# Turning attention outputs and q by DMA transposes in place of TensorE transposes

## The chip, the cores and the metric

The kernel runs on one core of one Trainium2 chip. The metric is the device time of one execution in microseconds; before the change three runs gave 191.22, 191.66 and 192.19 us, median 191.66 us. The profiled execution spans 190.9 us on the core.

## The reference: block attention with sorted keys, then a top-1 mixture of experts

There are B = 4 batches, H = 8 heads, S = 768 positions and head dimension D = 64. The sequence is cut into 8 blocks of 96. A small matrix P per batch and head (8 x 8, normalised five times over rows and columns) mixes the blocks of k and v. Each block of q then attends to the mixed block of the same number. The attention output, laid out as x of 3072 tokens by 512 features, goes to 8 experts, of which each token uses the best one.

```python
for _ in range(5):
    P = P - np.max(P, axis=-1, keepdims=True)
    P = np.exp(P)
    P = P / (np.sum(P, axis=-1, keepdims=True) + 1e-09)
    P = P / (np.sum(P, axis=-2, keepdims=True) + 1e-09)
k_sorted = np.einsum('bhij,bhjcd->bhicd', P, k_b)
v_sorted = np.einsum('bhij,bhjcd->bhicd', P, v_b)
scores = scale * np.matmul(q_b, k_sb.transpose(0, 1, 2, 4, 3))
attn = softmax(scores)
x = np.matmul(attn, v_sb)            # as (3072, 512)
logits = x @ w_gate                  # (3072, 8)
e = argmax(logits); gate = softmax(logits)[e]
out = gate * (np.maximum(x @ w1[e], 0.0) @ w2[e])
```

## The kernel before, in words

All matmul operands are bf16; the loads on GpSimd's DMA queue turn the fp32 inputs into bf16 on the way. TensorE does every matrix product and every transpose into PSUM, and VectorE or ScalarE copies results from PSUM to SBUF (`evac`, lines 254 to 258, where `engine`, line 246, chooses the engine with the smaller planned load).

The work of one batch has these parts.

- `turn_q` (line 265) turns q. Each batch has two pieces of 128 partitions (head, block and half block) by 24 x 64 columns. Twelve TensorE transposes of 128 x 128 per piece (line 269) fill a PSUM tile, and two copies per piece move it into `qT`.
- `sort_k` (line 291) and `sort_v` (line 312) apply P to k and v by matmuls with the matrices `pdiag`, and copy the results into `ksT` and `vs`. `sort_v` does two batches at a time.
- `attention` (line 375) goes over the 8 blocks. `scores` (line 333) does 16 matmuls of 64 rows by 48 columns into PSUM and one exponential on ScalarE over 768 columns into one of three `ex` tiles. `values` (line 355) does 8 matmuls with `ex` as the weights, and VectorE divides by the row sums into the tile `xo` (96 positions by 512 features; the pool has three of these). `turn` (line 372) does four TensorE transposes (line 378), and a copy puts the result into `xT`, features on partitions, for the whole batch. These three steps are staggered: in one pass of the loop block t gets its scores, block t - 1 its values and block t - 2 its turn. For the first four blocks of batch 0, four more transposes of the identity matrix (line 383) are issued as filler, which keep TensorE running.
- `route` (line 488) multiplies `xT` of a batch with the gate weights (line 493) and computes the expert's index and the gate on VectorE and ScalarE. It is called one pass after the last block's turn.
- `experts` (line 548) takes `xT` of a batch through the one expert whose weights were fetched. It does two halves of 384 tokens with 8 groups of 4 matmuls each (line 558), each followed by a relu from PSUM on VectorE or ScalarE, then 6 tiles of 128 tokens with 8 matmuls each (line 571), each followed by a scaled copy and a store to HBM from SyncE's queue (line 587).

The expert of a batch is guessed ahead from the sums of v (`predict`, `fetch`), so the weights are on their way long before the routing is known; a loop at the end redoes tokens for which the guess was wrong, and isn't entered when there are none.

The order of the instructions is written out by the program itself. Every part is a Python generator that yields an estimate in ns of the TensorE time it has issued (`T_Q`, `T_K`, `T_S`, ... in lines 262 and 263). `merge` (line 18) draws from two streams in proportion to their expected lengths: the experts of batch b, and beside them the q turn, k sort and attention of batch b + 1 (lines 652 to 669). Each engine then works through its own instructions in that order. Before the loop, `HEAD` passes of batch 0's attention are issued alone (line 632).

PSUM is shared by three tags with two buffers each: `s` (q, sorted k, scores, turned outputs), `v` (values) and `f` (experts and the small things). The q pieces have four buffers (`in_q`).

On GpSimd's DMA queue the order of loads is: q, v and k of batch 0 and v of batch 1; the first expert's weights; q and k of batch 1; the second expert's weights; v of batches 2 and 3; q and k of batch 2; and, from `look_ahead` (line 638) in the second pass of the main loop, the weights, q and k for the rest.

Of the kernel before, what the change touches and what calls it, by code (L numbers as in the profile page):

```python
# [9 lines left out]
BF16 = mybir.dt.bfloat16  # L10
# [31 lines left out]
def kernel(  # L42
# [11 lines left out]
    nc = tc.nc  # L54
# [7 lines left out]
    P = 128  # L62
# [64 lines left out]

    qT = [consts.tile([P, P, QC], BF16, name=f"qT{i}") for i in range(2)]  # L130
    ksT = [consts.tile([P, P * CW + 8], BF16, name=f"ksT{i}") for i in range(2)]
    ks3 = [t[:, :P * CW].rearrange("p (h c) -> p h c", c=CW) for t in ksT]
    vs = consts.tile([P, 2, HI, D + 2], BF16)
# [120 lines left out]
    def evac(dst, src, n, on=None):  # L254
        if (on or engine(n)) == "v":
            nc.vector.tensor_copy(dst, src)  # L256
        else:
            nc.scalar.copy(dst, src)  # L258

    T_Q, T_K, T_V, T_S, T_A, T_T = 680.0, 56.0, 89.0, 320.0, 380.0, 190.0
    T_1, T_2 = 650.0, 214.0

    def turn_q(b, on=None):
        for p in range(2):
            ps = psp.tile([P, 2, 8, P], BF16, tag="s")
            for u in range(CP // 2):
                nc.tensor.transpose(  # L269
                    out=ps[:, u // 6, u % 6, :],  # L270
                    in_=q_pieces[b][p][:, 2 * u:2 * u + 2, :].rearrange(
                        "p c d -> p (c d)"),
                    identity=ident)
            for g in range(2):
                c0 = p * (CP // 2) + g * 6
                evac(qT[b % 2][:, :, c0:c0 + 6],
                     ps[:, g, :6].rearrange("p c h -> p h c"), 768, on)
            yield T_Q

    def parts(total, alone):  # L280

# [9 lines left out]
    def sort_k(b):  # L291
        for w0, n, ps in parts(HC + 1, b == 0):
            for u in range(n):
                nc.tensor.matmul(  # L294
                    out=ps[:, u, :],
                    lhsT=k_in[b % 2][:, w0 + u:w0 + u + 2, :].rearrange(
                        "p c d -> p (c d)"),
                    rhs=pdiag[b].rearrange("p h i u -> p (h i u)"),
                    start=(u % 4 == 0), stop=(u % 4 == 3 or u == n - 1),
                    skip_group_check=True)  # L300
            evac(ks3[b % 2][:, :, w0:w0 + n],
                 ps[:, :n].rearrange("p c h -> p h c"), n * P)
            yield n * T_K
# [19 lines left out]
                 ps[:, :n].rearrange("p d h -> p h d"), n * P)  # L323
            yield n * T_V

    L_QK = 2 * T_Q + (HC + 1) * T_K
    L_V = D * T_V


# [3 lines left out]
    def scores(b, i):  # L333
        sc = psp.tile([P, 2, 512], F32, tag="s")
        for h in range(H):
            hi = h * NB + i
            for par in range(2):
                rows = slice(par * D, (par + 1) * D)
                k0 = hi * P + 1 - par
                nc.tensor.matmul(  # L340
                    out=sc[:, par, h * HC:(h + 1) * HC],
                    lhsT=ksT[b % 2][rows, k0:k0 + P],
                    rhs=qT[b % 2][rows, hi * U:(hi + 1) * U, :].rearrange(
                        "p u c -> p (u c)"),
                    start=(h == 0), stop=(h == H - 1), skip_group_check=True)
        ex = exs[n_ex[0] % len(exs)]
        n_ex[0] += 1
        nc.scalar.activation(  # L348
            ex[:, :H * BLK].rearrange("p (h t c) -> p t h c", t=2, c=HC),
            sc[:, :, :H * HC].rearrange("p t (h c) -> p t h c", c=HC),  # L350
            ACT.Exp, scale=scale)
        load["s"] += 810
        return ex
# [16 lines left out]
        return xo  # L370

    def turn(b, i, xo, fill):
        xf = xo.rearrange("p t g d -> p (t g d)")
        tp = psp.tile([P, 8, P], BF16, tag="f" if b == 0 else "s")
        tx = tp[:, :3].rearrange("p a c -> p (a c)").rearrange(
            "p (m c) -> p m c", c=BLK)
        for dc in range(DC):
            nc.tensor.transpose(out=tx[:, dc, :],  # L378
                                in_=xf[:, dc * P:(dc + 1) * P],
                                identity=ident[:BLK, :BLK])  # L380

        for f in range(fill):
            nc.tensor.transpose(out=tp[:, 4 + f, :], in_=ident, identity=ident)
        evac(xTs[b][:, :, i * BLK:(i + 1) * BLK].rearrange(
                 "p m (c t) -> p m c t", t=2),
             tx.rearrange("p m (t c) -> p m c t", t=2), 384)

    def attention(batches, fill):

        blocks = [(b, i) for b in batches for i in range(NB)]  # L390
        n = len(blocks)
        exq, xoq = {}, {}
        late = []
        for t in range(n + 3):
            if t < n:
                exq[t] = scores(*blocks[t])
                yield T_S
            if late:
                late.pop()()
            if 1 <= t <= n:  # L400
                xoq[t - 1] = values(*blocks[t - 1], exq.pop(t - 1))
                yield T_A
            if 2 <= t < n + 2:
                b, i = blocks[t - 2]
                if i == 0:
                    xT = keep.tile([P, DC, S], BF16, tag="xT")
                    xTs[b] = xT
                turn(b, i, xoq.pop(t - 2), fill if i < NB // 2 else 0)
                if i == NB - 1:
                    late.append(lambda b=b: route(b))  # L410
                yield T_T

# [133 lines left out]
    def experts(b, gwb, w, add):  # L548
        w1t, w2t = w
        xT = xTs[b]  # L550
        hTs = []
        for half in range(2):
            hT = ffn.tile([P, FC, NH], BF16, tag="hT")
            hTs.append(hT)
            for fc in range(FC):
                ps = psp.tile([P, NH], F32, tag="f")
                for dc in range(DC):
                    nc.tensor.matmul(  # L558
                        out=ps, lhsT=w1t[:, dc, fc * P:(fc + 1) * P],
                        rhs=xT[:, dc, half * NH:(half + 1) * NH],  # L560
                        start=(dc == 0), stop=(dc == DC - 1))
                if engine(NH) == "v":
                    nc.vector.tensor_scalar_max(hT[:, fc, :], ps, 0.0)  # L563
                else:
                    nc.scalar.activation(hT[:, fc, :], ps, ACT.Relu)  # L565
                yield T_1
        for t in range(NTB):
            hT, s = hTs[t // SUB], t % SUB
            ps = psp.tile([P, MD], F32, tag="f")
            for fc in range(FC):  # L570
                nc.tensor.matmul(  # L571
                    out=ps, lhsT=hT[:, fc, s * P:(s + 1) * P],
                    rhs=w2t[:, fc, :], start=(fc == 0), stop=(fc == FC - 1))
                if fc % 3 == 2:
                    yield 3 * T_2
            rows = slice(b * S + t * P, b * S + (t + 1) * P)
            o = ffn.tile([P, MD], F32, tag="o", bufs=3)
            if add:
                nc.sync.dma_start(out=o, in_=out[rows])
                nc.vector.scalar_tensor_tensor(  # L580
                    out=o, in0=ps, scalar=gwb[:, t:t + 1], in1=o,
                    op0=ALU.mult, op1=ALU.add)
            elif engine(MD) == "s":
                nc.scalar.activation(o, ps, ACT.Copy, scale=gwb[:, t:t + 1])  # L584
            else:
                nc.vector.tensor_scalar_mul(o, ps, gwb[:, t:t + 1])  # L586
            nc.sync.dma_start(out=out[rows], in_=o)
            yield 2 * T_2

    L_EXPERTS = 2 * FC * (T_1 + SUB * T_2)  # L590
    chosen = [None] * B
    tops = [None] * NPAIR

    def expert(b):
        yield from experts(b, gw[:, b], chosen[b], add=False)

    L_ATTEND = NB * (T_S + T_A + T_T)
    AHEAD = 0.88

    def attend(b, fill=0):  # L600
# [28 lines left out]
        load_k(2, p)  # L629
    idle_turns(1)  # L630
    main = attend(0, fill=4)
    HEAD = 3 * 6
    for _ in range(HEAD):
        next(main)
    spread(rep, 1, B)
# [16 lines left out]
    for b in range(B):  # L652
        steps, n = [], 0.0
        if b == 0:
            steps.append(lambda: main)
            n += L_ATTEND * 0.5
        if b + 1 < B:
            steps += [lambda: turn_q(b + 1), lambda: sort_k(b + 1)]
            n += L_QK
            if b + 1 == 2:  # L660
                steps.insert(0, look_ahead)
                steps.append(lambda: sort_v(1))
                n += L_V + 66 * 30.0
            steps.append(lambda: attend(b + 1))
            n += L_ATTEND
            merge((L_EXPERTS, expert(b)), (n / AHEAD, chain(*steps)))
        else:
            rest_i = count_others()
            run(expert(b))


    rv = nc.values_load(rest_i[0:1, 0:1], min_val=0, max_val=N)
    with tc.If(rv > 0):
        cur = consts.tile([P, 1], F32)
        nc.vector.memset(cur, float(E))
# [39 lines left out]
```

The softmax here doesn't subtract the row's maximum and nothing guards it: scores larger than these inputs give would overflow.

## Time and profile before

| what | us |
|---|---|
| device time, median of three | 191.66 |
| span of the profiled execution | 190.9 |
| TensorE busy | 158.1 (83%) |
| VectorE busy | 107.1 (56%) |
| ScalarE busy | 100.3 (53%) |
| GpSimd busy | 25.4 (13%) |
| loads on GpSimd's queue | 17.84 MB |
| stores and the first small load on SyncE's queue | 6.30 MB |

A busy time is the time in which at least one instruction of the engine ran. Matmuls overlap in TensorE's pipeline, so the mean of one matmul is longer than the step from one to the next. The chain that ended last is followed back from the last instruction, at each step to whatever released it, and its shares tell where a saved microsecond is one.

The stages by time: up to 31 us the inputs arrive, P is computed, and v and k of batch 0 are sorted. From 31.7 us the first blocks of attention run; the first expert matmul starts at 42.4 us. From there to 163.8 us the experts of batches 0, 1 and 2 run interleaved with the attention of the next batch (the first expert matmul of batch 1 is at 83.7 us), and the last 27 us are the experts of batch 3 alone.

### The profile page before, as it was taken

Reading aid. Unit: us, or ns where it says so; the run is one execution under the profiler, and the core shown is the slowest. Engines: PE = TensorE matmul, PEld = TensorE weight load, DVE = VectorE, ACT = ScalarE, POOL = GpSimd, SP = SyncE. Lnnn points to the kernel's source line nnn. Section 1 sums busy time; section 2 is a strip of 40 time slices with the busy share of each in tenths; the row PEclk is TensorE's granted clock in tenths of the full one; section 3 lists DMA queues with packets and bytes.
Section 4 is the critical chain, followed back from the end, with each engine's and each line's share of the span. In section 5 each row is a group of like instructions: output and inputs, shape, how many; then the busy total and the mean of one; then the engine's idle time right before and its main releaser. Section 6 shows DMA issues by size and latency. Waiting matters only on the chain.

```text
span 190.9 us, 4797 instructions
## 1 busy us (share of the span) xinstructions
PE 158.1 (83%) x2023; PEld 105.5 (55%) x2023; DVE 107.1 (56%) x308; ACT 100.3 (53%) x159; POOL 25.4 (13%) x51
## 2 busy tenths in 40 slices
PE   0342986987896999997889989989989999999990
PEld 0232975764664656555668845546756555555430
DVE  5870675879466767414754756763648656442210
ACT  5160478573775566533566466645776574434111
POOL 7960074122100000002900000000000000000000
PEclk9999999579999999999999999999999999999999
DMA  4999149999999993140999999713000122300332
GB/s 58 168 211 204 25 45 203 189 216 209 209 217 215 207 179 112 58 165 5 149 193 203 212 211 227 188 55 113 0 0 3 58 83 85 112 0 0 111 138 96
DMA packets 13211, 24.50 MB, mean 128 GB/s; under 512 B 1409, under 2 KB 5505, under 8 KB 13185
## 3 DMA queue, kind: packets, MB, share of 16 engines
q0 software_dynamic: 9680, 17.84, 52.2%
q1 hardware_dynamic: 3504, 6.30, 9.0%
q8 instruction: 18, 0.29, 0.6%
q14 instruction: 9, 0.07, 0.1%
HBM read 35.68 MB, written 6.29 MB: 220 GB/s over the span
## 4 chain that ended last, share of the span: by engine, by line
PE 62%; DVE 16%; ACT 9%; DMA 7%; issue 2%; POOL 1%; ACTq 0%; POOLq 0%
PE ps L571 19%; PE ps L558 18%; DMA v_in<-in_v_dram 7%; PE ps L316 6%; DVE xo L367 5%; PE sc L340 4%; PE ps L294 4%; PE av L361 4%; ACT ksT L258 3%; PE tp L378 2%; DVE ksT L256 2%; ACT qT L258 2%; DVE o L586 2%; DVE qT L256 1%; PE ps L439 1%
## 5 line engine op out<-in xcount | busy, mean ns | idle before, releaser
L558 PE MATMUL ps<-xT,w1t 128*128 128x384 bf16 x256 | 50.5, 326 | 1.4 <-ACT xT L258 0.9
L571 PE MATMUL ps<-w2t,hT 128*128 128x512 bf16 x192 | 48.7, 379 | 0.2
L563 DVE TENSOR_SCALAR hT<-ps 128x384 bf16<-128x384 f32 x37 | 20.6, 556 | 29.2 <-PE ps L558 29.0
L558 PEld LDWEIGHTS <-w1t 128*128 128x128 bf16 x256 | 23.0, 98 | 15.0 <-issue 4.0
L348 ACT ACTIVATE ex<-sc 128x768 bf16<-128x768 f32 x32 | 25.8, 814 | 10.0 <-PE sc L340 9.7
L367 DVE TENSOR_TENSOR xo<-av,rec 96x256 bf16<-96x256 f32 x64 | 26.9, 421 | 2.2
L571 PEld LDWEIGHTS <-hT 128*128 128x128 bf16 x192 | 15.8, 97 | 14.1 <-DVE sh L501 1.2
L565 ACT ACTIVATE hT<-ps 128x384 bf16<-128x384 f32 x27 | 13.3, 492 | 18.5 <-PE ps L558 18.4
L584 ACT ACTIVATE o<-ps,gw 128x512 f32<-128x512 f32 x15 | 10.3, 685 | 16.6 <-PE ps L571 15.4
L258 ACT COPY xT<-tp 128x384 bf16<-128x384 bf16 x29 | 13.8, 477 | 9.8 <-PE tp L378 8.4
L361 PE MATMUL av<-vs,ex 128*128 128x65 bf16 x256 | 15.6, 200 | 3.7 <-DVE rec L366 1.4
L258 ACT CAST ksT<-ps 128x1024 bf16<-128x1024 f32 (+2 forms) x18 | 16.1, 921 | 3.2 <-PE ps L294 3.0
L361 PEld LDWEIGHTS <-ex 128*128 128x128 bf16 x256 | 11.9, 101 | 9.7 <-DVE xo L367 2.7
L294 PE MATMUL ps<-pdiag,k_in 128*128 128x128 bf16 x196 | 14.8, 219 | 2.4 <-ACT vs L258 0.7
L294 PEld LDWEIGHTS <-k_in 128*128 128x128 bf16 x196 | 12.6, 98 | 5.3 <-issue 3.2
L269 PE MATMUL ps<-ident,t 128*128 128x128 bf16 x96 | 7.9, 242 | 8.7 <-DMA t<-in_q_dram 8.7
L366 DVE RECIPROCAL rec<-av 96x4 f32<-96x4 f32 x64 | 11.0, 171 | 6.9 <-PE av L361 6.7
L586 DVE TENSOR_SCALAR o<-ps,gw 128x512 f32<-128x512 f32 x9 | 6.8, 751 | 14.3 <-PE ps L571 14.3
L340 PE MATMUL sc<-qT,ksT 64*128 64x48 bf16 x512 | 12.1, 184 | 2.8 <-DVE ksT L256 1.3
L316 PEld LDWEIGHTS <-v_in 128*128 128x128 bf16 x128 | 13.5, 194 | 1.6 <-issue 0.9
L316 PE MATMUL ps<-pdiag_v,v_in 128*128 128x128 bf16 x128 | 13.6, 268 | 0.8 <-ACT ksT L258 0.8
L340 PEld LDWEIGHTS <-ksT 64*128 64x128 bf16 x512 | 8.8, 95 | 9.4 <-issue 6.7
(96 smaller groups left out, 148.4 us busy)
## 6 DMA issues: line engine op xcount, KB each, us to landing
out_dram<-o SPq DMA_DIRECT2D x24, 256.0 KB, 2.0
w1t<-in_moe_w_dram POOLq DMA_DIRECT2D x4, 1024.0 KB, 15.7
w2t<-in_moe_w_dram POOLq DMA_DIRECT2D x4, 1024.0 KB, 21.1
t<-in_q_dram POOLq DMA_DIRECT2D x8, 384.0 KB, 15.6
v_in<-in_v_dram POOLq DMA_DIRECT2D x4, 768.0 KB, 18.9
k_in<-in_k_dram POOLq DMA_DIRECT2D x8, 384.0 KB, 18.3
sn<-in_sort_net_dram SPq DMA_DIRECT2D x1, 8.0 KB, 1.5
wg<-in_moe_w_gate_dram POOLq DMA_DIRECT2D x1, 8.0 KB, 3.8
```

The source lines that it names most:

```text
L258: nc.scalar.copy(dst, src)
L294: nc.tensor.matmul(out=ps[:, u, :], lhsT=k_in[b % 2][:, w0 + u:w0 + u + 2, :].rearrange("p c d -> p (c d)"), rhs=pdiag[b].rearrange("p h i ...
L316: nc.tensor.matmul(out=ps[:, u], lhsT=v_in[:, :, :, d0 + u].rearrange("p u c -> p (u c)"), rhs=pdiag_v[g].rearrange("p h i -> p (h i)"), s ...
L340: nc.tensor.matmul(out=sc[:, par, h * HC:(h + 1) * HC], lhsT=ksT[b % 2][rows, k0:k0 + P], rhs=qT[b % 2][rows, hi * U:(hi + 1) * U, :].rear ...
L348: nc.scalar.activation(ex[:, :H * BLK].rearrange("p (h t c) -> p t h c", t=2, c=HC), sc[:, :, :H * HC].rearrange("p t (h c) -> p t h c", c ...
L361: nc.tensor.matmul(out=av[:, g, :], lhsT=ex[:, h * BLK:h * BLK + P], rhs=vs[:, b % 2, h * NB + i, :D + 1], start=(g == 0), stop=(g == 3), ...
L366: nc.vector.reciprocal(rec, av[:BLK, :, D:D + 1])
L367: nc.vector.tensor_mul(xo[:, half], av[:BLK, :, :D], rec.to_broadcast([BLK, 4, D]))
L558: nc.tensor.matmul(out=ps, lhsT=w1t[:, dc, fc * P:(fc + 1) * P], rhs=xT[:, dc, half * NH:(half + 1) * NH], start=(dc == 0), stop=(dc == DC ...
L563: nc.vector.tensor_scalar_max(hT[:, fc, :], ps, 0.0)
L565: nc.scalar.activation(hT[:, fc, :], ps, ACT.Relu)
L571: nc.tensor.matmul(out=ps, lhsT=hT[:, fc, s * P:(s + 1) * P], rhs=w2t[:, fc, :], start=(fc == 0), stop=(fc == FC - 1))
```

## The change

The attention outputs and the q of batches 1 to 3 are turned by transposing DMAs, from SBUF to SBUF on SyncE's queue, which also carries the output stores. It is meant to take the transposes off TensorE and the copies out of PSUM off VectorE and ScalarE. The q of batch 0 is still turned on TensorE.

[...] `qT` becomes `[P, QC, P]`, and the scores' right operand is read from it with a step. The exponential writes `ex` with the two halves of a block interleaved, so that the rows of `xo` come out in the order of the tokens. The turn yields no time of its own, the estimates `T_S` and `T_A` are a little smaller, and the routing moves from the end of the attention into the middle of the experts, after the first half.

```diff
-    qT = [consts.tile([P, P, QC], BF16, name=f"qT{i}") for i in range(2)]
+    qT = [consts.tile([P, QC, P], BF16, name=f"qT{i}") for i in range(2)]
...
-    T_Q, T_K, T_V, T_S, T_A, T_T = 680.0, 56.0, 89.0, 320.0, 380.0, 190.0
+    T_Q, T_K, T_V, T_S, T_A = 680.0, 56.0, 89.0, 300.0, 310.0
...
+    def flip_q(b):
+        for p in range(2):
+            c0 = p * (CP // 2)
+            nc.sync.dma_start_transpose(
+                out=qT[b % 2][:, c0:c0 + CP // 2, :],
+                in_=q_pieces[b][p].rearrange("p c d -> p (c d)"))
...
-                    rhs=qT[b % 2][rows, hi * U:(hi + 1) * U, :].rearrange(
-                        "p u c -> p (u c)"),
+                    rhs=qT[b % 2][rows, :, hi * U:(hi + 1) * U].rearrange(
+                        "p c u -> p u c"),
...
-            ex[:, :H * BLK].rearrange("p (h t c) -> p t h c", t=2, c=HC),
-            sc[:, :, :H * HC].rearrange("p t (h c) -> p t h c", c=HC),
+            ex[:, :H * BLK].rearrange("p (h c t) -> p h c t", h=H, t=2),
+            sc[:, :, :H * HC].rearrange("p t (h c) -> p h c t", h=H),
...
     def turn(b, i, xo, fill):
-        xf = xo.rearrange("p t g d -> p (t g d)")
-        tp = psp.tile([P, 8, P], BF16, tag="f" if b == 0 else "s")
...
-        for dc in range(DC):
-            nc.tensor.transpose(out=tx[:, dc, :],
-                                in_=xf[:, dc * P:(dc + 1) * P],
-                                identity=ident[:BLK, :BLK])
-
-        for f in range(fill):
-            nc.tensor.transpose(out=tp[:, 4 + f, :], in_=ident, identity=ident)
-        evac(xTs[b][:, :, i * BLK:(i + 1) * BLK].rearrange(
-                 "p m (c t) -> p m c t", t=2),
-             tx.rearrange("p m (t c) -> p m c t", t=2), 384)
+        nc.sync.dma_start_transpose(
+            out=xTs[b][:, :, i * BLK:(i + 1) * BLK],
+            in_=xo.rearrange("p t g d -> p (t g d)"))
+
+        if fill:
+            tp = psp.tile([P, 8, P], BF16, tag="f")
+            for f in range(fill):
+                nc.tensor.transpose(out=tp[:, f, :], in_=ident, identity=ident)
...
+            if half == 0 and not add:
+                route(b)
+                if b == B - 1:
+                    others.append(count_others())
+                yield 700.0
...
-    HEAD = 3 * 6
+    HEAD = 2 * 6
...
-            steps += [lambda: turn_q(b + 1), lambda: sort_k(b + 1)]
-            n += L_QK
+            flip_q(b + 1)
+            steps.append(lambda: sort_k(b + 1))
+            n += L_K
```

On SyncE's queue the order in the changed program is: the turns of blocks 0 to 3 of batch 0, the two halves of batch 1's q, the turns of blocks 4 to 7 of batch 0, then stores and turns in the order of the merge, with the q of batch 2 behind the last store of batch 0's experts and the q of batch 3 behind the last store of batch 1's.

## Prediction

> **What bounds the kernel now.** I first read the page's forty slices (each a fortieth of the span), the shares of the chain that ended last, then the groups with shapes kept apart.
>
> ```profile
> PE   0342986987896999997889989989989999999990
> PEclk9999999579999999999999999999999999999999
> DMA  4999149999999993140999999713000122300332
> ...
> PE 62%; DVE 16%; ACT 9%; DMA 7%; issue 2%; POOL 1%; ACTq 0%; POOLq 0%
> ```
>
> From about 42 us on TensorE is 90% busy or nearly so in almost every slice, at full clock, and it holds 62% of the chain. Instructions taken off TensorE there are worth nearly their own time. The DMA row is the other thing to see: it is full from about 31 to 72 us and from about 93 to 124 us, and almost empty elsewhere.
>
> ```profile
> L378 PE MATMUL tp<-ident,xo 96*128 96x96 bf16 x128 | 11.5, 214 | 0.9 <-ACT hT L565 0.4 <-DVE xo L367 0.3 <-DVE hT L563 0.2
> L269 PE MATMUL ps<-ident,t 128*128 128x128 bf16 x96 | 7.9, 242 | 8.7 <-DMA t<-in_q_dram 8.7
> L258 ACT COPY xT<-tp 128x384 bf16<-128x384 bf16 x29 | 13.8, 477 | 9.8 <-PE tp L378 8.4 <-PE tp L383 1.1
> L258 ACT COPY qT<-ps 128x768 bf16<-128x768 bf16 x12 | 9.2, 807 | 4.9 <-PE ps L269 2.6 <-DVE qT L256 2.3
> ```
>
> These are the rows that go. The means (214, 242 ns) are of pipelined matmuls and overlap; what one costs in a stream is read from the chain, whose columns are start, length, what:
>
> ```profile
> 48.10 0.34 PE tp L378 x4
> 48.47 0.49 ACT xT L258
> ...
> 49.64 0.59 PE lg L493 x24
> ...
> 130.63 0.67 PE ps L269 x12
> ```
>
> Twelve q transposes hold TensorE for 0.67 us, 56 ns each. Four output transposes take 0.34 us with their drain, about 0.2 us in a stream. And line 493, the gate of batch 0, can start at 49.64 only when the last copy into `xT` is done: all eight blocks of a batch must be turned before its routing.
>
> The last view is what the 16 DMA engines did in the half microsecond from 116.5 us (queue, packets, MB, share of the engines' time), and then, from the microsecond around its issue at 112.58 us, how long an output store took to land.
>
> ```profile
> q0 software_dynamic: 48, 0.05, 57.7%
> q1 hardware_dynamic: 44, 0.09, 52.8%
> ```
>
> ```profile
> out_dram<-o SPq DMA_DIRECT2D x1, 256.0 KB, 7.1
> ```
>
> Queue 0 carries the loads, queue 1 SyncE's stores. While both are active they take turns almost packet by packet (48 against 44). That store landed after 7.1 us; the median of the 24 stores is 2.0 us. Its first packet moved only 3.5 us after the issue.
>
> **What the skill says.** The Trainium skill, "DMA: Bandwidth & Descriptors", section "Queues, rings and completion order", says that each DMA engine goes round its rings at packet granularity. The trace agrees: 48 and 44. The same page, sections "SDMA does more than copy" and "DMA Transpose (X-bar)", describes the transpose in tiles with 256-byte source rows, 16 partitions by 128 columns at least. No run here shows one. Its section "Latency and other measured facts" gives 261 GB/s where the middle dimension isn't contiguous, which it puts down to descriptors that are not joined to 4 KB. I take that one, since our tiles are cut out of longer rows. Unmeasured here too. "SBUF — State Buffer", section "Door 1: The DMA port swizzle", says reads that touch a new 16-byte line each time pay a penalty; the trace has one such read, the strided weight loads of line 316, 194 ns against 98 ns for contiguous ones.
>
> **The change part by part.**
>
> *Removed from TensorE.* 72 q transposes (batches 1 to 3) at 56 ns: 4.0 us. 128 output transposes, 32 groups at 0.2 us: 6.4 us. The 16 filler transposes stay. Off ScalarE and VectorE: 29 x 477 + 3 x 549 ns = 15.5 us of `xT` copies and 12 of the 16 `qT` copies, some 10 us. Those engines are 56% and 53% busy, so this counts only where a TensorE group waits for its PSUM buffer, around 86 to 95 us for instance; I allow 2 us. Where the transposes are on time the gain is 4.0 + 6.4 + 2 = 12.4 us.
>
> *The scores' right operand* is now read with a step of 256 bytes. A pair of row-tiled matmuls takes 0.30/8 us = 37 ns now. If the strided read doubles a matmul, the cost is up to 0.3 us in each of 32 blocks, 9.6 us; at the other end it hides behind the weight loads. I take 0.05 us per block, 1.6 us: a pair is paced by two weight loads, and 48 columns at the 56 ns per 128 of the q transposes need only 21 ns. The exponential moves the same 768 elements, with the permutation in it: nothing, 814 ns is already set by the count. Route inside the expert stream: same 24 matmuls, no cost, but it now stands ahead of half 1 of the experts.
>
> *Added: transposes on SyncE's queue.* One block of output is 96 x 512, so 6 x 4 = 24 tiles, 98 KB; half a q is 128 x 1536, so 8 x 12 = 96 tiles, 393 KB. Sixteen rows over 16 engines make one 256-byte packet per engine and tile (my reading of the page). At 261 GB/s a 4 KB tile takes 15.7 ns: 0.4 us a block, 1.5 us a q half, plus the 2.0 us of the stores for issue and receipt. Where the DMA is free that is nothing: xT of batch 3 and the q of batches 2 and 3 are turned in free stretches (72 to 93, after 124), and three `xo` buffers cover 2.4 us.
>
> *But batch 0 and q of batch 1 fall in the full stretch.* If packets take turns, a transposed tile goes through only as a load packet does. The load packets by window of the before trace: 218 in 38 to 40 us, then 380, 504, 922, 376, 254 and 379 in the five-microsecond windows to 70, 71 after: 3104, or 194 per engine. Batch 0 and q of batch 1 need 8 x 24 + 2 x 96 = 384 tiles per engine. So queue 1 can't get through before the loads end, whatever the latency. The build order on SyncE is: blocks 0 to 3, both halves of q, blocks 4 to 7.
>
> - Blocks 0 to 3 need 96 packets: first data near 38 us (3.5 us after `xo` of block 0), 20 packets by 40, 24 by 45, 31 by 50, the rest by 52; landing near 54. The first expert matmul (line 558) stands at 42.4 now, so TensorE waits some 12 us there.
> - q of batch 1 and blocks 4 to 7 come behind. The loads, pushed back by 194 x 15.7 ns = 3 us, end near 75; then 190 tiles run at full rate. Block 7 has to wait until block 4's `xo` buffer is free. All of `xT` is down near 82 us. The gate of batch 0 stands at 49.6 now.
> - While it waits, TensorE can do half 0 and most of k's sort (about 4 us of what now lies after the gate) and nothing more, since it works in program order. From the gate to the last expert matmul of batch 0 there are now 84.2 - 49.6 = 34.6 us; less those 4, less 1.4 of q, 1.8 of output transposes and some 3 of idle time: 24.5. So batch 0 ends at 106.5 in place of 84.2: +22 us. A cold clock after the long wait (0.70 granted in 31 to 42 us) adds about 1.
> - Batches 1 to 3: the saving from 84 us on is 2.7 (q) + 3.4 (16 groups and drains) + 1.5 = 7.6 us. Against it the blocks of batch 2 under the second load stretch: 85 load packets per engine in 10 us (1357 in 110 to 120 us) make 24 tiles 2.8 us a block, where the pace is 1.95; some 4 us. And 1 us of strided scores.
>
> Sum: 191.7 + 22 + 1 - 7.6 + 4 + 1 = 212. The waits overlap other stalls in part and the packets need not alternate strictly, as 48 to 44 at the best place was for 2 KB packets; I go down to 208.
>
> **The rivals.**
>
> *Transposes keep pace (faster).* If descriptors are joined, or transposes don't wait behind loads, latency is 2.4 us and buffers cover it. 191.7 - 12.4 + 1.6 + 1 for a later start of the first expert = 182. For it: the DMA bytes are few (32 x 98 KB + 6 x 393 KB = 5.5 MB, about 21 us at 261 GB/s). Against: the 7.1 us store.
>
> *Latency, but not packet turns.* Each transpose in a full stretch pays the 3.5 us start and then moves fast, so 6 us. Block 3 lands near 47 (+5), three buffers at 6 us set a pace of about 2.2 us (+3 over batches 0 to 2): 191.7 - 12.4 + 1.6 + 5 + 3 = 189. For it: the store's data, once begun, went in 1.5 us. Against: those were 8 packets per engine, not 24 or 96.
>
> *Worse: transposes throttle the loads.* If all 16 engines must bring their row before a tile can go, each tile waits for the slowest and holds the others; the loads end near 85, and everything above moves by 10: 218.
>
> **How the numbers follow.** Packet turns 0.47, keep pace 0.22, latency only 0.17, worse 0.10, and 0.04 for parts that cancel within 0.5%. Likeliest: 208. The range runs from 182 to 216, leaving out the fast end of the second case and most of the worst. Faster is 0.22 + 0.14 of the latency case = 0.36; same 0.04; slower 0.60: 0.47, 0.10 and the rest of the latency case.
>
> **What would show it.** Right: queue 1 with some 20,000 more small packets; landing times of 10 us and more for the q halves issued before 72 us, about 2 to 4 us after; TensorE idle between about 42 and 80 us, waiting for `xT` and then line 487's gate; a full-speed tail that is shorter than before. Wrong: landing times of 2 to 4 us in 35 to 70 us, or few and large packets on queue 1. The scores' step shows in sixteen line-346 matmuls taking more than 0.30 us.

## The result and the profile after

The changed kernel takes 233.65 us (median of four, 232.68 to 234.72) where the kernel before took 191.93 in the same measurement: a ratio of 1.218, with an interval of 1.210 to 1.226. It is slower, and 25.7 us slower than the forecast of 208, outside its range. The profiled execution spans 232.9 us against 190.9. Executions of one kernel scatter, the slower ones at a lower granted clock, in some experiments too much for a ratio: these are given with their lowest and highest time.

First the page of the changed kernel: TensorE and its clock by fortieths (now 5.8 us each), the DMA row, queue 1, the shares of the chain, three groups, and the median landing times of the transposes.

```profile
PE   0419888030960098999998999468998999959990
PEclk9999995555597559999999999955899999997997
DMA  6994399999999800144999999983390124500132
...
q1 hardware_dynamic: 26224, 11.81, 23.9%
...
PE 52%; DMA 32%; DVE 7%; issue 2%; POOL 2%; ACT 2%; SPq 1%; POOLq 0%; DVEq 0%; ACTq 0%
...
L373 DVE TENSOR_TENSOR xo<-av,rec 96x256 bf16<-96x256 f32 x64 | 26.9, 420 | 38.0 <-DMA xT<-xo 36.0
...
L346 PE MATMUL sc<-qT,ksT 64*128 64x48 bf16 x512 | 26.7, 257 | 2.3 <-ACT hT L559 1.8
...
xT<-xo SPq DMA_TRANSPOSE x32, 2.3
qT<-t SPq DMA_TRANSPOSE x6, 5.8
```

TensorE stands still in slices 8 to 14 (41 to 81 us) except for two bursts, where the DMA row is full, and dips again in slice 26 (from 146 us), where the second stretch of loads runs. DMA has gone from 7% of the chain to 32%. VectorE, which writes `xo`, waited 36.0 us for earlier transposes to release their buffers. The medians, 2.3 and 5.8 us, look harmless, since most landings are outside the loads; the longest are 17.2 and 29.4 us. The scores' matmuls stayed the same 512 and went from 184 to 257 ns:

```profile
L340 PE MATMUL sc<-qT,ksT 64*128 64x48 bf16 x512 | 12.1, 184 | 2.8 <-DVE ksT L256 1.3
```

That was the kernel before. Now the chain of the changed kernel (start, length, what), with its long pieces:

```profile
43.78 29.44 DMA t<-in_q_dram
73.22 1.89 SPq L282
75.15 4.36 DMA xT<-xo
...
83.38 0.62 PE lg L487 x24
...
97.54 0.77 PE sc L346 x16
...
144.89 10.40 DMA xT<-xo
```

The gate of batch 0 is reached at 83.38 us, where it stood at 49.64. Before it lies one unbroken wait on transfers: the loads, during which q's transposes sit at the head of SyncE's queue, and after them the transposes of blocks 4 to 7. The name of the 29.44 us is inferred and misleads: the load that it names is one of batch 2's q, issued at 43.78, and nothing turned here reads that. What lasts as long is SyncE's issue of the two halves of batch 1's q:

```profile
48.30 26.81 SPq L282 DMA_TRANSPOSE qT<-t  x2
```

Block 4, whose `xo` was complete at 51.9 us, is issued behind them at 75.15. The piece at 144.89 is batch 2 in the second stretch of loads. What TensorE itself waited for in the first stretch is in its timeline, the wait in brackets:

```profile
58.19 1.44 PE L552 MATMUL ps<-xT,w1t 128*128 128x384 bf16 x4 [9.49 <-DMA xT<-xo]
81.08 1.44 PE L552 MATMUL ps<-xT,w1t 128*128 128x384 bf16 x4 [13.12 <-DVE hT L557]
```

The second line names a relu, though a relu takes 0.56 us and not 13. VectorE's timeline has the reason:

```profile
79.60 0.42 DVE L373 TENSOR_TENSOR xo<-av,rec 96x256 bf16<-96x256 f32 x1 [15.74 <-DMA xT<-xo]
...
80.49 1.01 DVE L557 TENSOR_SCALAR hT<-ps 128x384 bf16<-128x384 f32 x2
```

In VectorE's order these relus stand behind the `xo` of block 7, and that waits for the buffer that the turn of block 4 releases at 79.51 us. So a late transpose also stops expert matmuls that don't read it: TensorE had done seven of the eight groups of half 0, and the eighth waited for a PSUM buffer that such a relu frees.

And the DMA queues of the changed kernel between 60 and 65 us (packets, MB, share of the engines' time):

```profile
q0 software_dynamic: 190, 1.03, 100.9%
q1 hardware_dynamic: 189, 0.05, 7.7%
```

then between 77 and 79 us, when the loads are over:

```profile
q1 hardware_dynamic: 1942, 0.48, 116.3%
```

190 against 189: one packet of a transpose for each packet of a load, and the load packets are twenty times as large (5.4 KB against 256 bytes). In 50 to 55 us it is 519 to 520, in 55 to 60 748 to 745. Alone, the same queue moves 971 packets a microsecond (240 GB/s with its gaps, where the forecast reckoned with 261), against 38 between 60 and 65 us.

To see where the 42 us lie, I cut each profiled execution at the last second-layer matmul of each batch's expert, read from the chain (83.38, 129.98 and 163.65 us before; 112.74, 166.38 and 200.50 us in the changed kernel). Lengths in us; the last column is the span:

| kernel | head and batch 0 | batch 1 | batch 2 | batch 3 | span |
|---|---|---|---|---|---|
| before | 83.4 | 46.6 | 33.7 | 27.2 | 190.9 |
| changed | 112.7 | 53.6 | 34.1 | 32.4 | 232.9 |
| difference | +29.3 | +7.0 | +0.4 | +5.2 | +42.0 |
| forecast | +23 | +0.7 | -3.3 | 0 | +20.4 |

The forecast row divides its own terms: 22 + 1 for the head; of the saving of 7.6 us half for each of the two middle stages (each has one q, eight turns); 4 us for batch 2's turns, which run beside batch 1's expert; the 1 us of strided scores halved. The stage of batch 1 thus holds the turns of batch 2, and so on.

### The profile page after: what moved, and what is told of

It reads as the page before. It is cut to its first block, busy times and chain, and to the rows that moved or that the text cites. A ratio compares the mean times of both kernels' runs of the same rounds, so it can differ in the third digit from the quotient of the medians.

```text
span 232.9 us, 4482 instructions
## 1 busy us (share of the span) xinstructions
PE 169.4 (73%) x1823; PEld 109.2 (47%) x1823; DVE 95.3 (41%) x288; ACT 88.1 (38%) x135; POOL 25.5 (11%) x51
## 4 chain that ended last, share of the span: by engine, by line
PE 52%; DMA 32%; DVE 7%; issue 2%; POOL 2%; ACT 2%; SPq 1%; POOLq 0%; DVEq 0%; ACTq 0%
DMA t<-in_q_dram 19%; PE ps L570 18%; PE ps L552 16%; PE sc L346 7%; DMA xT<-xo 6%; DMA v_in<-in_v_dram 6%; PE ps L322 3%; PE ps L300 3%; PE av L367 2%; DVE xo L373 2%; DVE ksT L256 2%; PE ps L433 1%; DVE hT L557 1%; SPq L282 1%; ACT o L583 1%
## 5 line engine op out<-in xcount | busy, mean ns | idle before, releaser
L552 PE MATMUL ps<-xT,w1t 128*128 128x384 bf16 x256 | 53.8, 348 | 23.0 <-DVE hT L557 13.3
L570 PE MATMUL ps<-w2t,hT 128*128 128x512 bf16 x192 | 50.9, 402 | 0.0
L354 ACT ACTIVATE ex<-sc 128x768 bf16<-128x768 f32 x32 | 25.8, 810 | 51.1 <-PE sc L346 50.6
L557 DVE TENSOR_SCALAR hT<-ps 128x384 bf16<-128x384 f32 x26 | 14.4, 557 | 45.5 <-PE ps L552 45.3
L346 PE MATMUL sc<-qT,ksT 64*128 64x48 bf16 x512 | 26.7, 257 | 2.3 <-ACT hT L559 1.8
L559 ACT ACTIVATE hT<-ps 128x384 bf16<-128x384 f32 x38 | 18.4, 490 | 21.7 <-PE ps L552 21.7
L346 PEld LDWEIGHTS <-ksT 64*128 64x128 bf16 x512 | 19.9, 111 | 12.7 <-issue 10.6
L583 ACT ACTIVATE o<-ps,gw 128x512 f32<-128x512 f32 x18 | 12.4, 687 | 25.6 <-PE ps L570 23.7
L256 DVE CAST ksT<-ps 128x1024 bf16<-128x1024 f32 (+2 forms) x13 | 13.6, 1063 | 3.5 <-PE ps L300 3.4
L256 DVE CAST vs<-ps 128x1024 bf16<-128x1024 f32 (+1 forms) x8 | 8.2, 1022 | 10.8 <-PE ps L322 10.6
L532 POOL DMA_DIRECT2D w1t<-in_moe_w_dram x4 | 3.1, 770 | 82.7 <-DVE top L468 70.0
```

The source lines that it names most:

```text
L346: nc.tensor.matmul(out=sc[:, par, h * HC:(h + 1) * HC], lhsT=ksT[b % 2][rows, k0:k0 + P], rhs=qT[b % 2][rows, :, hi * U:(hi + 1) * U].rear ...
L354: nc.scalar.activation(ex[:, :H * BLK].rearrange("p (h c t) -> p h c t", h=H, t=2), sc[:, :, :H * HC].rearrange("p t (h c) -> p h c t", h= ...
L552: nc.tensor.matmul(out=ps, lhsT=w1t[:, dc, fc * P:(fc + 1) * P], rhs=xT[:, dc, half * NH:(half + 1) * NH], start=(dc == 0), stop=(dc == DC ...
L570: nc.tensor.matmul(out=ps, lhsT=hT[:, fc, s * P:(s + 1) * P], rhs=w2t[:, fc, :], start=(fc == 0), stop=(fc == FC - 1))
```

## The experiments

In the diffs, only the lines that matter.

**What the scores' step costs alone.** The kernel before, with the new layout of `qT`, so that scores read with a step of 256 bytes; everything else stays on TensorE.

```diff
-    qT = [consts.tile([P, P, QC], BF16, name=f"qT{i}") for i in range(2)]
+    qT = [consts.tile([P, QC, P], BF16, name=f"qT{i}") for i in range(2)]
...
-                    rhs=qT[b % 2][rows, hi * U:(hi + 1) * U, :].rearrange(
-                        "p u c -> p (u c)"),
+                    rhs=qT[b % 2][rows, :, hi * U:(hi + 1) * U].rearrange(
+                        "p c u -> p u c"),
```

> The kernel before, with q still turned on TensorE, but qT laid out as in the changed kernel and the scores' right operand read with its 256-byte step. Theory S (the step is costly: 16 score matmuls take 0.77 us in the trace of after against 0.30 us before, 0.47 us in each of 32 blocks): 15 us more, 206 to 208 us, with the 0.77 us again. As forecast (0.05 us a block): 193.5 us.

Measured: 204.27 us, ratio 1.062 (1.052 to 1.072). 12.3 us, not 1.6. The step costs on TensorE and on the path: sixteen score matmuls take 0.77 us in its chain and 0.30 in that of the kernel before. The stages grow by 6.7, 1.4, 3.7 and 0.4 us.

**What step is free.** The kernel before with q laid out so that neighbours lie 4 bytes apart.

```diff
-    qT = [consts.tile([P, P, QC], BF16, name=f"qT{i}") for i in range(2)]
+    qT = [consts.tile([P, HI, QC, U], BF16, name=f"qT{i}") for i in range(2)]
...
+                    rhs=qT[b % 2][rows, hi].rearrange("p c u -> p u c"),
```

> The kernel before with q on TensorE and the scores' right operand read with a step of 4 bytes (two elements) in place of 256: qT holds the two halves of a block interleaved. If a score matmul pays for each new 16-byte line, four successive columns share one and the time is near that of before, 16 matmuls in 0.30 to 0.45 us: 192 to 196 us. If any step other than one element costs the same, 0.77 us and 204 us.

Measured: 191.62 us, ratio 0.994 (0.991 to 0.997), sixteen matmuls in 0.30 us. So not any step costs. It is what the Trainium skill, "Advanced Engine Details and Errata", section "SBUF Cachelines", says: SBUF has lines of 16 bytes, an access to a different line each time is penalised, and at least two hits on a line are needed to hide it. With 4 bytes four elements fall on a line, with 256 one. This version is also the only one here faster than the kernel before, by 0.3 to 0.9%; what in it gains was not followed up.

**Which transposes hold up the head.** First the changed kernel with the q of all batches back on TensorE (and read without a step): only outputs go by DMA.

```diff
-            flip_q(b + 1)
-            steps.append(lambda: sort_k(b + 1))
-            n += L_K
+            steps += [lambda: turn_q(b + 1), lambda: sort_k(b + 1)]
+            n += L_QK
```

> The changed kernel with q of all batches on TensorE and the contiguous qT of before; only the attention outputs go by DMA. Packet turns: the 192 tiles of q leave the queue ahead of blocks 4 to 7, so the gate of batch 0 comes near 68 to 72 us in place of 83.4, and the scores fall back to 0.30 us; less 14, less 14, plus 5 for the q transposes: about 211 us. If the q tiles were not what holds blocks 4 to 7, the gate stays near 83 us: about 224 us.

Measured: 223.48 us, ratio 1.166 (1.158 to 1.173). The timeline of TensorE:

```profile
58.07 1.44 PE L546 MATMUL ps<-xT,w1t 128*128 128x384 bf16 x4 [9.43 <-DMA xT<-xo]
...
77.21 0.62 PE L481 MATMUL lg<-wg,xT 128*128 128x8 bf16 x8 [3.58 <-DMA xT<-xo]
```

Half the tiles of the stretch are gone (192 of 384 per engine), the packets still alternate (529 and 531 in 50 to 55 us), and yet the gate ends only 6 us earlier, at 77.8. The queue ran dry: blocks 3 and 4 wait for an `xo` buffer, and blocks 5 to 7 come only after 60 us, since TensorE stood before the first expert matmul, the first line above. From 60 to 65 us queue 1 moved 4 packets beside 199 of the loads. Blocks 5 to 7 then took 12 to 14 us to land. The count says why the gain is small: from 40 us to their end the loads have 2909 packets, 182 for each engine, so even 192 tiles last about as long as the loads, and turns that are missed are not made up for.

Then the other half: the kernel before, with q turned by DMA, outputs on TensorE.

```diff
-            steps += [lambda: turn_q(b + 1), lambda: sort_k(b + 1)]
-            n += L_QK
+            flip_q(b + 1)
+            steps.append(lambda: sort_k(b + 1))
+            n += L_K
```

> The kernel before with only the q of batches 1 to 3 turned by DMA, and the stepped scores; attention outputs stay on TensorE. Packet turns: 192 tiles per engine from about 47 us cannot be done before the loads end, q of batch 1 is down near 76 us where it is wanted at 61: 206 + 15 - 5 = 216 us. If a DMA transpose only paid a start of 3.5 us in the full stretch, q would be down near 52 us and the time is that of the stepped scores alone less the q transposes: about 202 us.

Measured: 219.1 us, ratio 1.142 (1.130 to 1.153). Its chain:

```profile
49.11 29.89 DMA qT<-t
```

q of batch 1 is down at 79 us, also with no other transposes in the queue, and TensorE waits 18.4 us for it. Either half alone keeps the head waiting until 77 to 79 us; undoing one gives little, since the other waits for the same loads.

**Does the wait follow the loads?** The changed kernel, with the loads of the second expert's weights, the later v, and q and k of batch 2 held back until the outputs of batch 0 are turned.

```diff
-    fetch(1, eid)
...
+    def late_loads():
+        nc.gpsimd.tensor_copy(hold, xTs[0][:, 0, S - 1:S])
+        fetch(1, eid)
+        for b in range(2, B):
+            load_v(b)
```

> The changed kernel with the loads behind k of batch 1 (weights of the second expert, v of batches 2 and 3, q and k of batch 2) held on their queue until block 7 of batch 0 is turned. Packet turns: with the queue of loads empty from about 48 us the tiles run at full rate, the gate of batch 0 comes near 55 us in place of 83.4, and the q halves land within 6 us; the loads held back take about 25 us more and are wanted from 85 us on: 208 to 212 us. If the transposes are slow by themselves and not because of the loads, the gate stays beyond 75 us and the time is not below 230 us.

Measured: 228.5 us, ratio 1.185 (1.173 to 1.197): a miss in the total, and a hit in the place. Its queues between 50 and 55 us, and then between 85 and 90 us:

```profile
q1 hardware_dynamic: 2794, 0.70, 74.4%
```

```profile
q0 software_dynamic: 361, 0.97, 98.0%
q1 hardware_dynamic: 360, 0.08, 12.9%
```

Without loads beside them the transposes go at once, and the gate comes at 62.6 us instead of 83.2. But the loads held back now meet the turns of batch 1, one packet for one, with a wait of 18.31 us in the chain from 74.45. Moving the loads moves the wait.

**More buffers.** The changed kernel with four `xo` tiles in place of three (`bufs=4`).

> The changed kernel with four xo buffers in place of three. Theory: in batch 2, VectorE waits for a buffer whose transpose sits behind loads (5.2, 2.6 and 0.8 us in the trace of after), and TensorE behind it; one more buffer puts the wait one block later, and in batch 0 block 7 needn't wait for block 4, so the gate comes near 80 us in place of 83.4: 3 to 7 us less, 227 to 231 us. If the buffers are not what passes the wait on, the same as after, 233 to 234 us.

Measured: 231.9 us, ratio 1.199 (1.190 to 1.209). About 2 to 4 us. In the head the buffer moves the wait and doesn't shorten it: TensorE now waits 10.0 us before the gate itself, whose last matmuls start at 82.2 us (83.2 with three buffers). What is gained lies in the stage of batch 1 (50.6 against 53.7), where batch 2's turns run beside loads.

**Shorter packets on the other side.** The changed kernel with the loads of q, k and v cut into pieces of 8 columns, so that there are more load packets to take turns with.

```diff
+        for c in range(0, CP, 8):
+            nc.gpsimd.dma_start(out=t[:, c:c + 8, :],
+                                in_=q_src[b, :, p * CP + c:p * CP + c + 8, :])
```

> The changed kernel with every load of q, k and v cut into DMAs of 8 columns (rows of 512 elements, 1 KB written), so that the same bytes come in up to six times as many packets. Packet turns: one tile goes through per load packet, so with smaller packets the tiles of batch 0 and of q go through faster per microsecond; the count of load packets per engine after 38 us is well over the 384 tiles, and the gate of batch 0 comes near 65 to 72 us in place of 83.4: 218 to 224 us. If the transposes get a share of the bytes, or wait for a fixed time each, the gate stays at 80 to 84 us and the time at 232 to 235 us.

Measured: 239.71 us (235.43 to 247.24), no ratio. The turns stay one for one (642 and 646 packets in 55 to 60 us), and the first q half lands in 20.2 us, not 29.4, as packet turns want it; the second takes 20.9, where it took 20.7. But GpSimd waits to issue so many transfers, the loads end over 10 us later, and the gate still stands at 81 to 86 us. The experiment changed two things and decides nothing about the total.

**The count in the last batch.** In the changed kernel, the count of tokens that go elsewhere moves behind the second half of the expert.

```diff
-                if b == B - 1:
-                    others.append(count_others())
...
+        if b == B - 1 and not add:
+            others.append(count_others())
```

> The changed kernel with the count of other tokens (batch 3) after half 1 of the experts in place of straight behind the gate. Theory: TensorE waits 2.45 us for the VectorE chain ahead of the count's one matmul and then runs 32 matmuls in 7.3 us in place of 5.2; both go: 229 to 231 us. If the slow half 1 has another cause, 231 to 232 us.

Measured: 230.12 us, ratio 1.191 (1.182 to 1.200), 3.5 us less by the medians. In the changed kernel TensorE, in program order, meets a matmul of the count that waits for VectorE's end of the routing, and the 32 matmuls behind it run at a lower clock:

```profile
209.52 0.17 PE L522 MATMUL tot<-restb,ones 128*128 128x1 bf16 x1 [2.45 <-DVE restb L520]
209.55 7.29 PE L552 MATMUL ps<-xT,w1t 128*128 128x384 bf16 x32
```

With the count later, the same 32 matmuls and the count behind them:

```profile
205.85 5.70 PE L552 MATMUL ps<-xT,w1t 128*128 128x384 bf16 x32
212.91 0.16 PE L522 MATMUL tot<-restb,ones 128*128 128x1 bf16 x1 [1.36 <-DVE restb L520]
```

The granted clock of 205 to 215 us is 1.00 in place of 0.83. A wait of 2.45 us cost about 1.6 us more in clock. The count isn't free in its new place either: TensorE waits 1.36 us for it ahead of the second layer.

**Do the parts add up?** From the runs above I had put 12 us on the step, 3.5 on the count and some 10 on batch 2. The three runs that follow take them out of the changed kernel one after another. First the step: q still comes by DMA, into `qraw`, and four copies a batch pack it for a step of 4 bytes, into one `qT` in place of two.

```diff
+    def pack_q(b):
+        for g in range(4):
+            c0 = g * 6
+            evac(qT[:, :, c0:c0 + 6, :],
+                 qraw[:, c0:c0 + 6, :].rearrange("p c (h u) -> p h c u", u=U), 768)
+            yield 1.0
...
+                    rhs=qT[rows, hi].rearrange("p c u -> p u c"),
```

> The changed kernel with one thing undone: q is still turned by DMA, but four copies per batch (VectorE or ScalarE, 768 columns each, about 0.8 us) pack it so that the scores read it with a 4-byte step. If the stepped read costs in the changed kernel what it cost alone (12.3 us), less about 1 us for the copies: 221 to 223 us, and sixteen score matmuls in 0.30 us. If much of it hides behind the waits for transposes: 227 to 231.

Measured: 233.1 us (227.2 to 236.06), no ratio: 0.5 us by the medians, 6 at the most, and by its stages (113.0, 53.3, 33.5, 32.6) 0.6 us. The profiles of the count later (without packing) and of the last of these three runs (with it) say the same: 111.7 and 111.4 us in the head, 34.1 and 33.2 in the stage of batch 2. My account of the 12 us falls. The scores are nearly as short as before:

```profile
PE 44%; DMA 35%; DVE 8%; ACT 5%; issue 3%; POOL 2%; SPq 1%; POOLq 0%; DVEq 0%; ACTq 0%
DMA t<-in_q_dram 19%; PE ps L560 16%; PE ps L578 15%; DMA xT<-xo 10%; DMA v_in<-in_v_dram 6%; PE ps L309 3%; DVE xo L381 3%; PE ps L331 3%; ACT qT L259 2%; PE sc L355 2%; PE av L375 2%; PE ps L441 1%; DVE ksT L257 1%; ACT ksT L259 1%; SPq L
...
L355 PE MATMUL sc<-qT,ksT 64*128 64x48 bf16 x512 | 13.1, 190 | 5.1 <-ACT qT L259 4.3
```

The scores' share of the chain falls from 7.0% to 2.2%, 11 us. In their place stand the waits for `xT`, from 6.3% to 9.9% (8 us), and the packing copies, 2.2% (5 us). Why the transposes now hold the path is in SyncE's timeline of this run:

```profile
95.32 2.48 SPq L387 DMA_TRANSPOSE xT<-xo  x2
100.73 0.37 SPq L594 DMA_DIRECT2D out_dram<-o  x1
101.19 3.86 SPq L387 DMA_TRANSPOSE xT<-xo  x2
```

No load is near. The queue issues in program order: from 97.8 to 100.73 us it is held by a store of the expert whose tile isn't ready, and a turn whose `xo` was complete at 99.0 goes out at 101.19, behind it. The chain then has `xT<-xo` for 4.09 us from 101.19. It isn't only the fast scores: the run with the count later, whose head is that of the changed kernel, has the same wait on its chain with slow scores (4.25 us from 99.75 us), and its head is 1.0 us shorter than the changed kernel's. The path through the scores and the path through SyncE's queue are about equally long, and shortening one leaves the other.

Then the count as well:

> The run with packed q, with the count of other tokens moved behind the second half of the experts as well. If costs add: 3.5 us below the run with packed q, 217 to 220. If not: the same as it.

Measured: 229.39 us, ratio 1.177 (1.163 to 1.192). Stages 110.9, 53.8, 33.3, 30.3: the last is 2.3 us shorter, as it was without packing (32.4 to 29.8); by the medians the whole is 3.7 us less. In its own stage this part does add.

Then batch 2's outputs on TensorE:

```diff
     def turn(b, i, xo, fill):
+        if b == 2:
...
+            for dc in range(DC):
+                nc.tensor.transpose(out=tx[:, dc, :],
+                                    in_=xf[:, dc * P:(dc + 1) * P],
+                                    identity=ident[:BLK, :BLK])
+            evac(xTs[b][:, :, i * BLK:(i + 1) * BLK], tx, 384)
+            return
```

> The last run, with the outputs of batch 2 turned on TensorE (eight groups of 0.2 us, 1.6 us more of TensorE). If the stall of batch 2 behind the second stretch of loads is worth the 10 us in the chain: 8 us less, 209 to 212, and what is then left over the kernel before is the wait of batch 0 and of batch 1's q alone. If only the forecast 4 us: 214 to 218.

Measured: 221.04 us, ratio 1.144 (1.132 to 1.156). The stage of batch 1 falls from 53.8 to 43.6 us (53.4 with the count later and no packing), about 10 us, to 3 less than in the kernel before; the other stages stay within 0.5. By their ratios the two runs differ by 6 us. With the 1.6 us that TensorE took on, batch 2's turns cost 8 to 12 us beside the second loads.

**Transposes only where the DMA is idle.** The kernel before, with DMA turns for blocks 4 to 7 of batch 1 and all of batch 3, routing between the halves, the count later, four `xo` tiles.

```diff
+    def by_dma(b, i):
+        return b == 3 or (b == 1 and i >= 4)
```

> The kernel before with DMA transposes only where the loads are over: outputs of blocks 4 to 7 of batch 1 and of all of batch 3; q and all the rest on TensorE with the contiguous qT; route inside the experts after half 0, the count of other tokens after half 1; four xo buffers. Theory: 12 groups of four transposes leave TensorE (0.2 us each, 2.4 us) and nothing waits, since a transpose lands in 2.3 us there: 188.5 to 190 us. If DMA transposes cost time even without loads beside them: 192 us or more.

Measured: 195.6 us, ratio 1.013 (1.010 to 1.016). The transposes landed in 2.3 to 4.0 us, and it is still slower. Its chain has

```profile
81.90 2.26 DMA out_dram<-o
```

and the same again, 2.10 us, at 152.88: output tiles waiting to be stored. Each transpose occupies SyncE's queue for about 1.2 us where a store takes 0.33, and the stores stand behind three of them. But cut as above, the stages are 83.4, 46.5, 33.6 and 30.9 us, where they were 83.4, 46.6, 33.7 and 27.2: in the stages with DMA turns, waits and savings cancel. The whole loss is in the last, where no transpose runs, and where this version has the routing and the count. To take the stores out, they went to GpSimd's queue; beside it the same with the layout for a step of 4 bytes, and the kernel before with that edit alone.

```diff
-            nc.sync.dma_start(out=out[rows], in_=o)
+            (nc.sync if add else nc.gpsimd).dma_start(out=out[rows], in_=o)
```

> The kernel with DMA transposes where the loads are over, and the output stores issued from GpSimd's queue in place of SyncE's. Theory: there, the stores stood in SyncE's queue behind transposes that hold it for 1.2 us each, and VectorE waited 7.1 us for an output buffer; apart from them the stores don't wait: 3 to 5 us less than 195.6, 189 to 192 us. If the loss has another cause: 195 to 196 us.

> The same with q in the interleaved layout that the scores read with a 4-byte step (0.6% faster by itself): 1 us less than the run with stores on GpSimd's queue, 188 to 191 us. If the two gains overlap, the same as that run.

> The kernel before with its output stores issued from GpSimd's queue, nothing else changed. No store waits in SyncE's queue before the change, so the same time, 191 to 193 us; if stores gain from that queue by themselves, less than 190 us, and the transposes have no part in it.

Measured: 195.84 (ratio 1.015, 1.008 to 1.021), 195.24 (1.011, 1.004 to 1.018) and 196.15 us (1.015, 1.008 to 1.021). The gains expected of the first two did not come, since the stores from GpSimd, against the third expectation, cost 1.5% in a kernel without one DMA transpose (they land in 2.4 us instead of 2.0), most of it at the end. That kernel's profile ends 8.1 us after its last matmul, instead of 5.0. Up to the last matmul the move did help the version with DMA turns, 185.5 us against 187.7. Set against the third run, DMA turns in idle stretches gain 0.3 us, nothing that can be measured: by stages 82.0, 45.7, 33.6 and 32.5 against 84.1, 46.6, 33.7 and 30.3, a small gain before and a loss in the stage with the routing. These are single profiles of programs whose times scatter by 2 to 3 us. None of these versions pays; DMA turns in idle stretches with the routing left where it was were not run.

## Why the prediction was wrong

- **Packet turns, right.** Queue 1 has 22,720 more packets (some 20,000 forecast), beside loads one per load packet; the q halves land in up to 29 us; the first expert matmul stands at 58.2 after a wait of 9.5 us (54 and 12 forecast), the gate at 83.4 (82). The loads end near 76 us (75): the case "transposes throttle the loads", whose 218 is nearer to the result, is not what happened. That the packets "need not alternate strictly", one of two reasons for going from 212 down to 208, did not happen: those 4 us were given away. The Trainium skill's "DMA: Bandwidth & Descriptors", section "Queues, rings and completion order", says that an engine takes turns between its rings at packet granularity; that the sizes of the packets don't matter, from 1.1 to 5.4 KB beside 256 bytes, is what the trace adds.
- **After the gate of batch 0**, 24.5 us were to be left; it took 29.4, and this step failed. I subtracted what TensorE no longer has to do and took it that the rest stays as long. On the chain eight blocks of scores take 0.77 us each in place of 0.30, 3.8 us. Beside that path runs another of about the same length, through turns that stand behind stores on SyncE's queue, so without the step the stage is no shorter. I had named who is queued behind a transpose in the loads, and not what a transpose is queued behind. (My 84.2 us for the end of batch 0's experts before is 0.8 us too late; it enters both sides and cancels.)
- **"The scores' right operand … I take 0.05 us per block, 1.6 us"** is a step that failed. It is 0.47 us a block (0.77 against 0.30), beyond even the 0.3 that I gave as the upper end, and 12.3 us in the kernel before. The pace that I took from two weight loads does not hold: with the step a pair takes 96 ns, not 37. In the changed kernel taking the step out gives almost nothing, because other waits come forward. It fits the stage of batch 2, where +0.4 us was measured and -3.3 forecast, a gap as large as the 3.7 us that the step alone cost in that stage. But packing gave only 0.6 to 0.9 of it back there; the copies and a wait of 4.61 us for `xT` took its place.
- **"The blocks of batch 2 under the second load stretch … some 4 us"** is the step that failed most: 8 to 12. I spread the packets evenly over the stretch and gave a block 2.8 us; the first three took 8.0, 10.4 and 9.3 us to land. They hold the three `xo` buffers, so the fourth block stops, TensorE idles from 148.3 to 152.2 us, the clock drops (0.53 in 156 to 166 us), and the expert's matmuls interleaved with the attention wait in program order. A late block cost its wait and the clock after it: 13 matmuls of the second layer take 4.66 us there, and 2.82 in the next batch.
- **"Route inside the expert stream: same 24 matmuls, no cost"**: this step failed too. The tail that was to be shorter than before is 5.2 us longer, and 2.6 us of that (3.5 by the medians) go when the count behind the route moves. I counted instructions and not whom they wait for. Of the rest, 1.36 us are TensorE's wait for the count in its new place and 0.6 the gate's matmuls, which the stage didn't have before; what is left was not taken apart.
- **The savings** are there where nothing else holds the path: with batch 2 on TensorE and no step, the stage of batch 1 is 3.0 us shorter than before; the q transposes that left it are 24 x 56 ns, 1.3 us. That the rest is from their copies and buffers, as the forecast had it, was not shown.

By stages the forecast of 212 was short by 6.3 in the head, 6.3 in batch 1's stage, 3.7 in batch 2's and 5.2 in the last; with the 4 us taken off for the 208 that is the whole of the miss. The mechanism, packet turns, was right. Four sizes around it were too small, and all on the same side; in three of them (after the gate, batch 2, the route) I counted work and left out waits, and the fourth, the step, I sized without a measurement.

What stays open: how the 29.4 us after the gate divide between step, queue order and packing, since each removal brought the next limit forward, and stores on a queue that costs nothing were not found. How much of each loss is the clock, which is 0.87 over the whole execution where it was 0.98 and drops where TensorE waited, was not separated. The shorter head of the order (`HEAD`) and the smaller estimates, which are part of the change, were not tried alone.

## What to carry to other kernels

Before moving work to DMA transposes, look at the DMA row where they would run and count packets: here each 256-byte piece waited for a whole load packet of up to 5.4 KB, so the transposes lasted as long as the loads, and holding the loads back only moved the wait. Check the order on the issuing queue in both directions, what waits behind a transpose and what it waits behind, and on every engine that fills or frees its buffers: a relu behind a late `xo` held up the experts. And don't add up costs that were measured one at a time: 12.3 us of slower matmuls were worth 0.5 us by the medians once transfers set the pace, so take a suspect out of the changed kernel before blaming it.

## What the hardware showed that was not expected

- A moving operand read with a step of 256 bytes takes 0.77 us for sixteen matmuls of 64 rows by 48 columns, against 0.30 us with a step of 4 bytes or none.
- One packet each for two queues that both had work, whatever their sizes: 190 to 189 with 5.4 KB against 256 bytes, 748 to 745 with 1.1 KB; alone, the transposes ran at 1942 packets in 2 us.
- A transpose of 96 x 512 occupies SyncE's queue for 1.2 us, one of 128 x 1536 for 1.5 us, and beside loads for up to 16.7 us; a store for 0.33 us.
- Stores issued from GpSimd in place of SyncE cost 1.5% (1.008 to 1.021) with nothing else changed; the profile ends 8.1 us after the last matmul, in place of 5.0.
